# Softmax attention with a gated unit on one core: single score banks for VectorE, gate jobs that wait for weights, numbered PSUM banks in setup

## The chip, the cores and the metric

The kernel runs on one core of a Trainium2 chip. A core has TensorE (PE; its weight loads are a row of their own, PEld), VectorE (DVE), ScalarE (ACT), GpSimd (POOL) and SyncE (SP), each with its own instruction queue in program order, and 16 DMA engines. TensorE writes into PSUM, eight banks of 128 partitions x 512 floats. The metric is the device time of one execution in microseconds; what is shown is the median of three runs.

## The reference

The inputs are x (2048 x 640, bf16), the weights wqkv (640 x 1920) and wo (640 x 640) of an attention with 32 heads of 20 columns, and w_gate, w_up (640 x 1728) and w_down (1728 x 640).

```
xn  = layernorm(x)
q, k, v = split(xn @ wqkv)                      # 32 heads, 20 columns each
p   = softmax(q k^T / sqrt(20))                 # 2048 x 2048 for each head
s   = concat_heads(p v) @ wo
h   = sigmoid(xn @ w_gate) * (xn @ w_up)
g   = silu(h @ w_down)
out = x + s * g
```

The largest part is the softmax: 32 x 2048 x 2048 exponentials.

## The kernel before

**Setup.** Sixteen tiles of 128 rows of x are normalised, transposed on TensorE and copied to xnT. From it come K and q for the first group of four heads, and the first V tiles. The engines' order is a list of words written out by hand, ORDER: `tr.5` transposes tile 5, `k.2` multiplies a part of K, `kadd.2:DVE` evicts chunk 2 of K on VectorE, `qbound` and `qT` finish q. PSUM tiles come from rotating tags (`tp` with four buffers, `k` with three, `q` with one); `keep_clock` (L233) multiplies zeros into q's bank.

**Main part.** There are 32 passes: four chunks of 512 queries times eight groups of four heads. A pass has 64 *score banks* (16 key tiles x 4 heads), 128 keys x 512 queries each, so there are 2048 in all. A bank becomes exponentials in one of two ways:

- ScalarE takes them in *rounds*, three banks and two banks in turn (tiles `sc0` and `sc1`, five PSUM banks), one instruction each (L1166).
- VectorE takes one bank at a time, the tile `spare`, in four instructions (L1177, L1182, L1186, L1190): a bit trick with a cubic. In the program before, such a bank is issued only inside `issue()`, together with a ScalarE round, when less than 2500 ns of planned work lies before VectorE.

The exponentials are multiplied with V into the bank `oacc` (L1278, eight matmuls a batch, `P8` below). At the end of a pass `normalise` copies `oacc`, sends the denominators through DRAM and scales.

The two banks `misc0` and `misc1` are shared by `spare` and by all other products, the *jobs*: K, V and q of later groups, the bounds that keep the exponents in range (`bound_job`), gate and up (`gateup_job`, 56 of them), down, and the output. Jobs are generators; each yields what it needs next: a bank, a matmul, or a condition.

**What sets the order.** When the program is built, a planner walks through time. It keeps a time for TensorE (`pe[0]`) and queues with costs for ScalarE and VectorE, and at each step issues the next ScalarE round when it is due, else a batch with V, else a job's matmul, else a product with zeros that only keeps TensorE busy (`zero_add`, L1254). Nothing of this runs on the chip: what it leaves is each engine's fixed order and the semaphore waits for data and buffers. In the lists below a token such as `S3` or `S2` is a ScalarE round of that many score matmuls, `X1` a bank for VectorE. In the last pass a bank takes two matmuls of 256 queries, so the tokens read `S6` and `S4`.

**Weights of gate and up.** `load_glu` asks for the next job's weights on SP's queue when a job starts (two buffers each, `WB = 2`).

**The end.** The last pass is split into two halves of 256 queries. `last_job` handles the first half beside the last rounds: correction products (L855), VectorE's L868 and sums (L871). After the last exponential, VectorE copies the accumulator (L804), and a chain of a reciprocal, two small matmul steps and the last products ends with the output's DMA.

Of the kernel before, what the change touches and what calls it, by code (L numbers as in the profile page):

```python
# [9 lines left out]
FP32 = mybir.dt.float32  # L10
# [5 lines left out]
P = 128  # L16
# [21 lines left out]
apply.10 scale.14 apply.11 tr.7 stats.12 xnT.6 apply.14 less.12:DVE xnT.9 tr.10 xnT.7 sqrt.12  # L38
scale.12 tr.8 tr.11 xnT.10 xnT.11 k.1 xnT.8 apply.12 tr.14 stats.15 apply.13 tr.12 kmax.1
less.15:DVE sqrt.15 scale.15 xnT.14 xnT.12 tr.13 k.2 kmax.0 apply.15 kadd.0 tr.15 xnT.13:DVE xnT.15  # L40
k.3 k.4 qabs kmax.2 v.1 kmax.3 v.3 kmax.4 kmost v.0 kbound vd.1 vd.0 qbound kadd.1 table kadd.3:DVE
vd.3 v.2 vd.2 qT kadd.2:DVE
"""

LOG2E = 1.4426950408889634
# [13 lines left out]
def kernel(  # L59
# [99 lines left out]
    def v_matmuls(ps, tiles, h0, h1):  # L159
        n = (h1 - h0) * Dh  # L160
        for k, tt in enumerate(tiles):
            for kd in range(KD):
                nc.tensor.matmul(ps[:, k * n:(k + 1) * n], lhsT=xnT[:, kd, tt * P:(tt + 1) * P],  # L163
                                 rhs=wv[:, kd, h0 * Dh:h1 * Dh], start=(kd == 0), stop=(kd == KD - 1),
                                 skip_group_check=True)
                yield

    def v_copy(ps, tiles, h0, h1):
        n = len(tiles)
        nc.vector.tensor_copy(  # L170
            out=v_all[:, tiles[0]:tiles[0] + n, h0:h1, 1:1 + Dh],
            in_=ps[:, 0:n * (h1 - h0) * Dh].rearrange("p (t h e) -> p t h e", t=n, e=Dh))
# [3 lines left out]
    with tc.tile_pool(name="setup", bufs=1) as sp, \  # L176
# [53 lines left out]
        WARM, AFTER = 12, {0: 2, 1: 6, 2: 2, 3: 2, 4: 2, 5: 2}  # L230
        tps, kps, vps, first = {}, {}, {}, {}

        def keep_clock(n):  # L233
            if "idle" not in first:
                first["idle"] = ps0.tile([P, 512], FP32, tag="q", bufs=1, name="unused")
            for _ in range(n):
                nc.tensor.matmul(first["idle"].rearrange("p (k c) -> p k c", c=P), lhsT=zero,
                                 rhs=zero.unsqueeze(1).to_broadcast([P, 4, P]), start=True, stop=True)

        def copy(other, home, out, in_):  # L240
# [35 lines left out]
                                    scalar2=rstd[:, t:t + 1], op0=ALU.add, op1=ALU.mult)  # L276

        def transpose(t, other):
            tps[t] = ps0.tile([P, KD, P], BF16, tag="tp", bufs=4, name="tp")
            for kd in range(KD):  # L280
                nc.tensor.transpose(out=tps[t][:, kd, :], in_=x_sb[:, t, kd * P:(kd + 1) * P], identity=ident)
            keep_clock(AFTER.get(t, 0))

        def xnT_evict(t, other):
            copy(other, "ACT", xnT[:, :, t * P:(t + 1) * P], tps[t])
# [1 line left out]
        def k_mm(i, other):  # L287
            c, a, b = K_PARTS[i]
            if not a:
                kps[c] = ps0.tile([P, 512], FP32, tag="k", bufs=3, name="ps_k")  # L290
            first_matmuls(kps[c][:, a:b], wkp, slice(c * 512 + a, c * 512 + b))

        def k_part_max(i, other):
# [12 lines left out]
                                           op0=ALU.mult, op1=ALU.min)  # L306

        def v_mm(t, other):
            ps = ps0.tile([P, KD, P], BF16, tag="tp", bufs=4, name="ps_v")
            vps[t] = ps.rearrange("p k d -> p (k d)").bitcast(FP32)  # L310
            for _ in v_matmuls(vps[t], range(t, t + 1), 0, VF):
                pass

        def q_mm(t, other):
            first["ps"] = ps0.tile([P, 512], FP32, tag="q", bufs=1, name="ps_q")
            first_matmuls(first["ps"], wqp, slice(0, QC))

        def q_bound(t, other):
# [3 lines left out]
        def q_evict(t, other):  # L322
# [7 lines left out]
              "kmost": lambda t, other: k_most(DENSE, parts=len(K_PARTS)), "kbound": k_bound, "q": q_mm,  # L330
              "qabs": lambda t, other: first.update(abs=q_abs(first["ps"])), "qbound": q_bound,
              "table": lambda t, other: nc.scalar.activation(out=warm[:, 1:2], in_=eps_t, func=ACT.Exp),
              "qT": q_evict, "v": v_mm, "vd": lambda t, other: v_copy(vps[t], range(t, t + 1), 0, VF)}
        keep_clock(WARM)
        for word in ORDER.split():
            name, _, other = word.partition(":")
# [104 lines left out]
    def take_bank(name="work"):  # L441
        ready = [i for i in range(2) if banks[i].t is not None and banks[i].t <= pe[0]]
        if not ready:
            return None
        i = min(ready, key=lambda i: banks[i].t)
        banks[i] = Cell()
        return i, psum.tile([P, QC], FP32, tag=f"misc{i}", bufs=1, name=name)
# [7 lines left out]
    def give_bank(held, cell):  # L455
        banks[held] = cell
# [144 lines left out]
        next_pad[0] += 1  # L601
        return True

    glu_w = {}

    def load_glu(c, kf):
        fsz, f0 = fsz_list[kf], kf * P
        wg = glu[0].tile([P, KD, P], BF16, tag="wg", bufs=WB, name="wg")
        nc.sync.dma_start(out=wg[:, :, 0:fsz], in_=B_w_gate[:, f0:f0 + fsz].rearrange("(kd p) f -> p kd f", p=P))
        wu = glu[0].tile([P, KD, P], BF16, tag="wu", bufs=WB, name="wu")  # L610
        nc.sync.dma_start(out=wu[:, :, 0:fsz], in_=B_w_up[:, f0:f0 + fsz].rearrange("(kd p) f -> p kd f", p=P))
        glu_w[c, kf] = (wg, wu)

    hTs, h_cells, d_cells = {}, {}, {}

    def gateup_job(c, kf):
        fsz = fsz_list[kf]
        if kf == 0 and c:
            yield "known", lambda: len(d_cells.get(c - 1, [])) == QC // P
        elif kf:  # L620
            yield "known", lambda: c in hTs
        hT_free = d_cells[c - 1] if c and not kf else []
        n = c * NFT + kf + WB - 1
        if n < NQC * NFT:
            load_glu(n // NFT, n % NFT)
        wg, wu = glu_w.pop((c, kf))
        if kf == 0:
            hTs[c] = glu[0].tile([P, NFT, QC], BF16, tag="hT", bufs=1, name="hT")
        hT = hTs[c]
        cols = slice(c * QC, (c + 1) * QC)  # L630
        held, psg = yield "bank",
        for kd in range(KD):
            nc.tensor.matmul(psg[0:fsz, :], lhsT=wg[:, kd, 0:fsz], rhs=xnT[:, kd, cols],  # L633
                             start=(kd == 0), stop=(kd == KD - 1))
            yield "mm", MM5
        made = {}

        def gate():
            made["t"] = wk.tile([P, QC], BF16, tag="tnh", bufs=2, name="tnh")
            nc.scalar.activation(out=made["t"][0:fsz, :], in_=psg[0:fsz, :], func=ACT.Tanh, scale=0.5)  # L640

        gated = act.add(480.0, [Cell(pe[0] + PE_OUT + 100.0), *tnh_free[-2:-1]], gate, 0, EXP_LAG)
        give_bank(held, gated)
        held, psu = yield "bank",
        for kd in range(KD):
            nc.tensor.matmul(psu[0:fsz, :], lhsT=wu[:, kd, 0:fsz], rhs=xnT[:, kd, cols],  # L646
                             start=(kd == 0), stop=(kd == KD - 1))
            yield "mm", MM5
        tnh_free.append(dve.add(600.0, [Cell(pe[0] + PE_OUT), gated, *hT_free],
                                lambda: nc.vector.scalar_tensor_tensor(  # L650
                                    out=hT[0:fsz, kf, :], in0=made["t"][0:fsz, :], scalar=1.0,
                                    in1=psu[0:fsz, :], op0=ALU.add, op1=ALU.mult), 1))
        give_bank(held, tnh_free[-1])
        h_cells.setdefault(c, []).append(tnh_free[-1])
# [413 lines left out]

    KEEP_SPARE, KEEP_LATE, SPARE_END, next_round = 800.0, 400.0, 20 * PER_PASS, [0.0]
    BUFS, D_BACKLOG = {3: 4, 2: 4, 1: 3}, 2500.0  # L1070
    NEEDED, NEEDED_LAST = 6, 12
    PV_TIME = 2 * MM5 + 30.0
    sets = [Cell(0.0), Cell(0.0)]
    buffers = {n: [Cell(0.0)] * BUFS[n] for n in BUFS}
# [23 lines left out]
    def lacks():  # L1098
        return list({(w[1], w[2]): w for b in coming(GH) for w in needs(b)}.values())
# [8 lines left out]
    def dve_bank(banks):  # L1108
        b = min((x for x in coming(GH) if x not in banks), default=None)
        if b is None:  # L1110
            return None
        ends = PER_PASS * (b // PER_PASS + 1) if b < LAST else min(e for e in ENDS if e > b)
        if ends - b > (NEEDED if ends < NB else NEEDED_LAST):
            return b
        if ends == NB:
            return None
        b = ends + b % GH
        while b // GH in done_ahead[b % GH]:
            b += GH
        cells = [w[0].get(w[1]) for w in needs(b)]  # L1120
        if any(c is None or c.t is None or c.t > pe[0] for c in cells):
            return None
        return b
# [76 lines left out]
    def issue():  # L1200
# [23 lines left out]
        at_bank[0] += n  # L1224
        return n

    def pv_batch():

        p = pv_pass[0]
        if p >= len(steps) - 1 + len(PARTS):  # L1230
            return None
        if sum(pv_count[0]) == 0 and not (oacc_free[0].t is not None and oacc_free[0].t <= pe[0]):
            return None
        batch = []
        for j in range(GH):
            mine = []
            for x in ready_p[j]:
                b, buf, i = x
                if unit(b) > p or len(mine) == 2:
                    break  # L1240
                c, v = buf.made, v_cells.get((b % PER_PASS // GH, steps[min(p, len(steps) - 1)][1]))
                if c.t is not None and c.t + SEM <= pe[0] and v is not None and v.t is not None and v.t <= pe[0]:
                    mine.append(x)
            if len(mine) < 2:
                return None
            batch.append(mine)
        return batch
# [61 lines left out]
    while pv_pass[0] < len(steps) - 1 + len(PARTS):  # L1309
# [25 lines left out]
                continue  # L1335
        room = until - pe[0]
        next_round[0] = until
        held = sum(len(q) for q in ready_p)
        batch = pv_batch()
        cost = PV_TIME + (INTO["pv"] if mode[0] != "pv" else 0.0)  # L1340
# [102 lines left out]
```

## Time and profile before

| | |
|---|---|
| median of 3 runs | 891.46 us (891.35 to 891.49) |
| profiled execution, its own time | 894.59 us |
| its span | 892.9 us |
| TensorE busy | 813.2 us (91%) |
| VectorE busy | 839.8 us (94%) |
| ScalarE busy | 869.8 us (97%) |
| GpSimd busy | 162.6 us (18%) |
| granted TensorE clock, mean | 0.995 |
| DMA | 64.40 MB, 72 GB/s |

A group's line gives line, engine, operation, output and input with their shapes, the count, then the busy time and the mean duration of one, and then the engine's idle time just before these instructions, with what ended most of it. Busy time merges instructions that overlap, so it can be less than count times duration. Instruction times are from the span's start. A clock of 1.00 is TensorE's full speed.

### The profile page before, as it was taken

To read this page: it belongs to the slowest core of one execution; us is meant where nothing else is said; L and a number is where in the kernel's file an instruction comes from. 1 tells how busy PE (TensorE), PEld (TensorE's weight loads), DVE (VectorE), ACT (ScalarE), POOL (GpSimd) and SP (SyncE) were. 2 spreads that over 40 slices of the span, in tenths; PEclk is the share of its full clock that TensorE was granted. 3 is DMA by queue.
4 is the path that set the end of the run, shared out by engine and by line. 5 is a ranking of instruction groups with operands and counts; after the bars stand their busy time and mean duration, and the time that the engine had idled before them with its cause. 6 is when DMAs were issued, how large, how long until landed. Compare 5 with 4: busy or idle time off the path is not lost.

```text
span 892.9 us, 16976 instructions
## 1 busy us (share of the span) xinstructions
PE 813.2 (91%) x6259; PEld 291.3 (33%) x6343; DVE 839.8 (94%) x1482; ACT 869.8 (97%) x835; POOL 162.6 (18%) x311
## 2 busy tenths in 40 slices
PE   8899999999989899999899998989999898999896
PEld 3344333232223333232233332223333332233333
DVE  7799999999999999997999999999999989999997
ACT  7799999999999999999999999999999999999995
POOL 8401111011111212111101221101112220111121
PEclk9899999999999999999999999999999999999999
DMA  8113231135451134223202243303113433200012
GB/s 318 40 34 96 61 112 35 51 98 140 117 137 42 59 90 68 70 58 72 63 23 79 62 89 79 71 25 78 33 44 86 108 53 71 67 18 20 14 32 72
DMA packets 107673, 64.40 MB, mean 72 GB/s; under 512 B 80350, under 2 KB 101906, under 8 KB 107498
## 3 DMA queue, kind: packets, MB, share of 16 engines
q1 hardware_dynamic: 97382, 47.21, 19.9%
q0 software_dynamic: 10208, 16.11, 7.9%
q8 instruction: 49, 0.80, 0.4%
q14 instruction: 34, 0.28, 0.1%
HBM read 50.45 MB, written 16.13 MB: 75 GB/s over the span
## 4 chain that ended last, share of the span: by engine, by line
ACT 59%; issue 17%; PE 12%; DVE 8%; DMA 2%; POOL 0%; SPq 0%; DVEq 0%; ACTq 0%; POOLq 0%
ACT p L1166 55%; PE sc L1144 4%; ACT tnh L640 3%; DVE dy L1177 2%; PE oacc L1278 2%; PE work L137 2%; DVE du L1182 1%; DMA wqd<-in_A_wqkv_dram 1%; PE work L633 1%; DVE p L1190 1%; PE work L669 1%; ACT td L680 1%; DVE du L1186 1%; DMA den<-den_dram 0%; PE work L163 0%
## 5 line engine op out<-in xcount | busy, mean ns | idle before, releaser
L1166 ACT ACTIVATE p<-sc 128x1536 bf16<-128x1536 f32 x717 | 828.7, 1358 | 6.1 <-PE spare L1144 2.5
L1144 PE MATMUL sc<-qT,kT_all 21*128 21x512 bf16 (+1 forms) x1848 | 280.8, 377 | 57.4 <-ACT p L1166 48.1
L1177 DVE TENSOR_SCALAR dy<-spare 128x512 f32<-128x512 f32 x257 | 175.6, 684 | 24.7 <-PE spare L1144 22.2
L1144 PEld LDWEIGHTS <-kT_all 21*128 21x128 bf16 x2112 | 90.4, 91 | 288.3 <-issue 275.0
L1186 DVE SCALAR_TENSOR_TENSOR du<-du,dy 128x512 f32<-128x512 f32 x257 | 174.5, 682 | 1.7
L1190 DVE SCALAR_TENSOR_TENSOR p<-du,dy 128x512 uint16<-128x512 f32 x257 | 174.3, 681 | 1.4
L1182 DVE SCALAR_TENSOR_TENSOR du<-dy 128x512 f32<-128x512 uint16 x257 | 174.5, 683 | 0.8
L1278 PE MATMUL oacc<-p,v_all 128*21 128x512 bf16 (+1 forms) x2112 | 158.0, 377 | 0.6 <-DVE v_all L170 0.3
L1144 PE MATMUL spare<-qT,kT_all 21*128 21x512 bf16 (+1 forms) x264 | 99.0, 379 | 0.0
L762 POOL DMA_DIRECT2D den_dram<-oev x31 | 18.1, 584 | 392.6 <-DVE oev L761 392.6
L669 PE MATMUL work<-wd,hT 128*128 128x320 bf16 x448 | 85.5, 302 | 0.1
L633 PE MATMUL work<-xnT,wg 128*128 128x512 bf16 (+1 forms) x261 | 77.6, 383 | 1.9 <-issue 0.6
L646 PE MATMUL work<-xnT,wu 128*128 128x512 bf16 (+1 forms) x268 | 73.1, 381 | 1.2 <-DVE dy L1177 0.3
L778 POOL DMA_DIRECT2D rl<-rec_dram x124 | 62.1, 514 | 60.2 <-DMA rec_dram<-den 51.0
L1254 PE MATMUL oacc<-xnT,zero 128*128 128x512 bf16 x165 | 56.5, 387 | 3.5 <-issue 2.7
L1278 PEld LDWEIGHTS <-v_all 128*21 128x21 bf16 x2112 | 31.2, 90 | 62.6 <-issue 60.7
L669 PEld LDWEIGHTS <-hT 128*128 128x128 bf16 x448 | 35.0, 97 | 48.6 <-issue 39.1
L640 ACT ACTIVATE tnh<-work 128x512 bf16<-128x512 f32 (+1 forms) x56 | 41.2, 735 | 0.0
L650 DVE SCALAR_TENSOR_TENSOR hT<-tnh,work 128x512 bf16<-128x512 bf16 (+1 forms) x56 | 38.0, 678 | 2.2 <-ACT tnh L640 2.2
L772 POOL DMA_DIRECT2D rec_dram<-den x31 | 17.0, 549 | 123.0 <-DVE den L771 118.4
L708 PE MATMUL work<-wo_pad,oT 128*128 128x320 bf16 x192 | 35.6, 302 | 0.5 <-issue 0.5
L633 PEld LDWEIGHTS <-wg 128*128 128x128 bf16 (+1 forms) x280 | 21.7, 98 | 42.8 <-issue 31.1
(128 smaller groups left out, 562.5 us busy)
## 6 DMA issues: line engine op xcount, KB each, us to landing
wg<-in_B_w_gate_dram SPq DMA_DIRECT2D x52, 160.0 KB
wu<-in_B_w_up_dram SPq DMA_DIRECT2D x52, 160.0 KB
rl<-rec_dram POOLq DMA_DIRECT2D x124, 64.0 KB, 2.3
qT<-q_dram SPq DMA_DIRECT2D x31, 128.0 KB
gq_dram<-d POOLq DMA_DIRECT2D x12, 320.0 KB, 2.5
gqr<-gq_dram SPq DMA_DIRECT2D x12, 320.0 KB
kT_all<-k_dram SPq DMA_DIRECT2D x28, 128.0 KB
wd<-in_B_w_down_dram SPq DMA_DIRECT2D x13, 160.0 KB
```

What stands on the lines that cost most here:

```text
L633: nc.tensor.matmul(psg[0:fsz, :], lhsT=wg[:, kd, 0:fsz], rhs=xnT[:, kd, cols], start=(kd == 0), stop=(kd == KD - 1))
L640: nc.scalar.activation(out=made["t"][0:fsz, :], in_=psg[0:fsz, :], func=ACT.Tanh, scale=0.5)
L646: nc.tensor.matmul(psu[0:fsz, :], lhsT=wu[:, kd, 0:fsz], rhs=xnT[:, kd, cols], start=(kd == 0), stop=(kd == KD - 1))
L669: nc.tensor.matmul(psd[:, 0:HALF], lhsT=hT[0:fsz, kf, t4 * P:(t4 + 1) * P], rhs=glu[1][0:fsz, kf, e0_:e1_], start=(kf == 0), stop=(kf == N ...
L778: nc.gpsimd.dma_start(out=t["rl"][32 * j:32 * j + 32, :], in_=rec_dram[n, j:j + 1, :].to_broadcast([32, QC]))
L1144: nc.tensor.matmul(ps[:, c0:c0 + n], lhsT=kT_all[rows, g, kt * P:(kt + 1) * P], rhs=qTs[qc, g][rows, q0:q0 + n], start=True, stop=True, ti ...
L1166: nc.scalar.activation(out=buf.tile(), in_=ps, func=ACT.Exp, bias=EXP_BIAS, scale=exp_scale)
L1177: nc.vector.tensor_scalar(out=t["y"], in0=ps, scalar1=LEAST, scalar2=None, op0=ALU.max)
L1182: nc.vector.scalar_tensor_tensor(out=t["u"], in0=t["f"], scalar=CUBE_2, in1=t["f"], op0=ALU.add, op1=ALU.mult)
L1186: nc.vector.scalar_tensor_tensor(out=t["u"], in0=t["u"], scalar=CUBE_1, in1=t["f"], op0=ALU.add, op1=ALU.mult)
L1190: nc.vector.scalar_tensor_tensor(out=buf.tile()[:, 0, :].bitcast(U16), in0=t["u"], scalar=CUBE_SCALE, in1=t["y"], op0=ALU.mult, op1=ALU.add)
L1278: nc.tensor.matmul(oacc[32 * j:32 * j + 1 + Dh, q0:q0 + width], lhsT=v_all[:, kt, GH * g + j, 0:1 + Dh], rhs=buf.ap[:, i, c0:c0 + width], ...
```

## The change

Three things change.

1. A new function `alone` in the main loop. When the next round is not yet due, VectorE has less than 700 ns of planned work, and K, q and a PSUM bank are there, one score bank is issued for VectorE on its own, outside a ScalarE round.
2. A gate and up job waits, in the planner, until 4000 ns after its weights were asked for.
3. In setup each PSUM tile has a numbered bank: K's chunks take banks 0, 3, 1 and 0, the transposes and V take 4, 2, 5 and 6 in turn, q takes 7. V's first four tiles are made in two pairs instead of one by one. ORDER changes in its last two lines only: among others the copy of K's chunk 2 moves ahead of `qbound`, and four products with zeros into the bank of K's chunk 1 are added (`idle.3`, `idle.1`).

```diff
-k.3 k.4 qabs kmax.2 v.1 kmax.3 v.3 kmax.4 kmost v.0 kbound vd.1 vd.0 qbound kadd.1 table kadd.3:DVE
-vd.3 v.2 vd.2 qT kadd.2:DVE
+k.3 k.4 qabs kmax.2 kmax.3 kmax.4 v.0 idle.3 kmost kbound vd.0 kadd.2:DVE kadd.3:DVE qbound v.2
+idle.1 vd.2 kadd.1 table qT
...
-        def keep_clock(n):
-            if "idle" not in first:
-                first["idle"] = ps0.tile([P, 512], FP32, tag="q", bufs=1, name="unused")
+        K_BANKS, T_BANKS, Q_BANK = (0, 3, 1, 0), (4, 2, 5, 6), 7
+
+        def bank(n, name, dtype=FP32):
+            ps = ps0.tile([P, 512], FP32, tag=f"b{n}", bufs=1, name=name)
+            return ps if dtype == FP32 else ps.bitcast(dtype)[:, 0:D].rearrange("p (k c) -> p k c", c=P)
+
+        for n in range(8):
+            bank(n, "home")
+
+        def keep_clock(n, at=Q_BANK):
+            unused = bank(at, "unused")
...
-            for _ in v_matmuls(vps[t], range(t, t + 1), 0, VF):
+            vps[t] = bank(T_BANKS[t // 2], "ps_v")
+            for _ in v_matmuls(vps[t], range(t, t + 2), 0, VF):
...
-        glu_w[c, kf] = (wg, wu)
+        glu_w[c, kf], glu_t[c, kf] = (wg, wu), pe[0] + LANDED
...
             yield "known", lambda: c in hTs
+        yield "known", lambda: pe[0] > glu_t.get((c, kf), 1e18)
         hT_free = d_cells[c - 1] if c and not kf else []
...
+    def alone(room):
+        if (chunk[0] < 2 or (0.0 if mode[0] == "score" else INTO["score"]) + MM5 > room
+                or dve.backlog + max(0.0, dve.t - pe[0]) >= ALONE or any(c.t is None for c in d_made[-2:-1])):
+            return False
+        if any(w[0].get(w[1]) is None or w[0][w[1]].t is None or w[0][w[1]].t > pe[0] for w in lacks()):
+            return False
+        b = dve_bank([])
+        held = take_bank("spare") if b is not None else None
+        if held is None:
+            return False
+        pe_do("score", 0.0)
+        begun = pe[0]
+        score(held[1], b)
+        issued(b)
+        give_bank(held[0], dve_exp(held[1], b, begun))
+        pe_do("score", MM5)
+        at_bank[0] += 1
+        return True
...
         room = until - pe[0]
         next_round[0] = until
+        if b0 < NB and not stuck and alone(room):
+            idle = False
+            credit = min(credit + per_bank(b0), 3000.0)
+            continue
```

More of the change, by code (lines that the diff above doesn't have):

```diff
@@ L231 @@
         tps, kps, vps, first = {}, {}, {}, {}
-        def keep_clock(n):
-            if "idle" not in first:
-                first["idle"] = ps0.tile([P, 512], FP32, tag="q", bufs=1, name="unused")
+        K_BANKS, T_BANKS, Q_BANK = (0, 3, 1, 0), (4, 2, 5, 6), 7
[6 more added lines that the diff above has]
+            unused = bank(at, "unused")
             for _ in range(n):
-                nc.tensor.matmul(first["idle"].rearrange("p (k c) -> p k c", c=P), lhsT=zero,
+                nc.tensor.matmul(unused.rearrange("p (k c) -> p k c", c=P), lhsT=zero,
                                  rhs=zero.unsqueeze(1).to_broadcast([P, 4, P]), start=True, stop=True)
@@ L278, in transpose @@
         def transpose(t, other):
-            tps[t] = ps0.tile([P, KD, P], BF16, tag="tp", bufs=4, name="tp")
+            tps[t] = bank(T_BANKS[len(tps) % 4], "tp", BF16)
             for kd in range(KD):
                 nc.tensor.transpose(out=tps[t][:, kd, :], in_=x_sb[:, t, kd * P:(kd + 1) * P], identity=ident)
-            keep_clock(AFTER.get(t, 0))
+            if t in AFTER:
+                keep_clock(AFTER[t])
         def xnT_evict(t, other):
@@ L289, in k_mm @@
             if not a:
-                kps[c] = ps0.tile([P, 512], FP32, tag="k", bufs=3, name="ps_k")
+                kps[c] = bank(K_BANKS[c], "ps_k")
             first_matmuls(kps[c][:, a:b], wkp, slice(c * 512 + a, c * 512 + b))
@@ L308, in v_mm @@
         def v_mm(t, other):
-            ps = ps0.tile([P, KD, P], BF16, tag="tp", bufs=4, name="ps_v")
-            vps[t] = ps.rearrange("p k d -> p (k d)").bitcast(FP32)
-            for _ in v_matmuls(vps[t], range(t, t + 1), 0, VF):
+            vps[t] = bank(T_BANKS[t // 2], "ps_v")
+            for _ in v_matmuls(vps[t], range(t, t + 2), 0, VF):
                 pass
         def q_mm(t, other):
-            first["ps"] = ps0.tile([P, 512], FP32, tag="q", bufs=1, name="ps_q")
+            first["ps"] = bank(Q_BANK, "ps_q")
             first_matmuls(first["ps"], wqp, slice(0, QC))
@@ L332 @@
               "table": lambda t, other: nc.scalar.activation(out=warm[:, 1:2], in_=eps_t, func=ACT.Exp),
-              "qT": q_evict, "v": v_mm, "vd": lambda t, other: v_copy(vps[t], range(t, t + 1), 0, VF)}
+              "qT": q_evict, "v": v_mm, "vd": lambda t, other: v_copy(vps[t], range(t, t + 2), 0, VF),
+              "idle": lambda t, other: keep_clock(t, K_BANKS[1])}
         keep_clock(WARM)
@@ L602, in pads @@
         return True
-    glu_w = {}
+    glu_w, glu_t = {}, {}
     def load_glu(c, kf):
@@ L1070 @@
     BUFS, D_BACKLOG = {3: 4, 2: 4, 1: 3}, 2500.0
-    NEEDED, NEEDED_LAST = 6, 12
+    NEEDED, NEEDED_LAST, ALONE = 6, 12, 700.0
     PV_TIME = 2 * MM5 + 30.0
```

## The prediction

> **What bounds the kernel now.** I read the page's busy table and costliest groups, then busy time by stretches, then ScalarE's idle stretches in the timeline, then the two ends of the run.
>
> ```profile
> PE 813.2 (91%) x6259; PEld 291.3 (33%) x6343; DVE 839.8 (94%) x1482; ACT 869.8 (97%) x835; POOL 162.6 (18%) x311
> L1166 ACT ACTIVATE p<-sc 128x1536 bf16<-128x1536 f32 x717 | 828.7, 1358 | 6.1 <-PE spare L1144 2.5
> L1177 DVE TENSOR_SCALAR dy<-spare 128x512 f32<-128x512 f32 x257 | 175.6, 684 | 24.7 <-PE spare L1144 22.2
> L633 PE MATMUL work<-xnT,wg 128*128 128x512 bf16 (+1 forms) x261 | 77.6, 383 | 1.9 <-issue 0.6
> ```
>
> ScalarE is the bound: 717 exponential rounds hold 828.7 us of it. VectorE takes 257 single banks beside them (four instructions each) and waits 22.2 us for scores. The gate matmuls wait 1.9 us in all, and almost none of it for weights.
>
> ```profile
> 0.00:28.65 28.65, 22.69 (x161) 11.58 (x164) 22.01 (x72) 21.23 (x47) 24.34 (x59) 1.00 0.69 248
> 28.65:100.00 71.35, 66.10 (x536) 27.78 (x542) 66.52 (x119) 67.25 (x59) 8.38 (x18) 0.95 0.20 56
> 300.00:400.00 100.00, 92.95 (x711) 33.11 (x722) 97.40 (x169) 99.73 (x93) 19.93 (x35) 1.00 0.32 75
> 700.00:800.00 100.00, 90.21 (x677) 30.44 (x687) 90.22 (x153) 100.00 (x96) 18.33 (x32) 1.00 0.30 62
> 880.00:893.00 13.00, 5.66 (x47) 2.84 (x44) 7.84 (x16) 2.15 (x3) 0.40 (x1) 0.89 0.26 76
> ```
>
> The columns after the length are PE, PEld, DVE, ACT, POOL, the granted clock, DMA share and GB/s. From 128 us to 882 us ScalarE is full; nothing but fewer rounds shortens that stretch. Before it lie 28.65 us of setup and a start with holes, behind it a tail of 10.7 us. ScalarE's holes, one line for each stretch of it, the idle time before it in brackets:
>
> ```profile
> 28.65 2.37 ACT L1166 ACTIVATE p<-sc 128x1536 bf16<-128x1536 f32 x2 [1.56 <-PE sc L1144]
> 31.31 2.52 ACT L1166 ACTIVATE p<-sc 128x1536 bf16<-128x1536 f32 x2 [0.30 <-PE spare L1144]
> 35.68 8.54 ACT L1166 ACTIVATE p<-sc 128x1536 bf16<-128x1536 f32 x7 [1.84 <-PE spare L1144]
> 48.01 12.40 ACT L1166 ACTIVATE p<-sc 128x1024 bf16<-128x1024 f32 x11 [1.26 <-PE oacc L1278]
> ```
>
> With smaller ones (0.16, 0.40, 0.28, and 0.23 at 317 us) the holes after the first round make 4.47 us. The next rows show why two of them are there (PE busy time, instructions, then the clock):
>
> ```profile
> 23.40:26.80 3.40, 2.78 (x30) 1.00 0.00 0
> 26.80:30.20 3.40, 2.04 (x11) 0.98 0.06 14
> 30.20:33.60 3.40, 3.07 (x11) 0.50 0.11 19
> 33.60:37.00 3.40, 3.40 (x19) 0.52 0.12 36
> ```
>
> TensorE was busy 2.04 of 3.40 us at the hand-over from setup; then its clock was half for 6.8 us, and the holes of 0.30 and 1.84 us fall there.
>
> **The change part by part.** Counts are from the instruction order of the two built programs.
>
> *Rounds.* The new branch issues a bank for VectorE with no ScalarE round beside it. The programs have 13 such banks, and 249 beside rounds instead of 257: 262 in all, 5 more. ScalarE has 357 rounds of three banks and 357 of two instead of 358 and 358. A pair holds ScalarE for 828.7 / 358.5 = 2.31 us (durations of 1.573 and 1.145 us overlap). All of it lies on the path: **-2.31 us**. VectorE gets 5 x (0.684 + 0.683 + 0.682 + 0.681) = 13.65 us more. From 28.65 to 880 us it is busy 810.0 of 851.4 us by the stretches, so 41.4 us are free and 27.8 stay free. The cover is thinnest from 300 to 400 us, with 2.6 us free; about that stretch is rounds 240 to 320 (one in 1.19 us), which get 160 VectorE instructions instead of 157, so 2.0 us. TensorE has room: the zero products that only keep its clock fall from 215 to 185, 30 x 0.22 us (the spacing in a row of five, 1.25 us less 0.39 for one, over four) = 6.5 us, and in 132 places it waits 48.1 us for ScalarE. Cost there: nothing.
>
> *First round.* Before, the first scores wait for two VectorE evictions of K:
>
> ```profile
> 26.39 0.69 ACT L324 ACTIVATE qT<-ps_q,e_one 128x512 bf16<-128x512 f32 x1 [0.39 <-POOL v_all L346]
> 27.36 0.74 DVE L300 TENSOR_SCALAR kT_all<-ps_k,e 128x512 bf16<-128x512 f32 x1
> 28.16 0.39 PE L1144 MATMUL sc<-qT,kT_all 21*128 21x512 bf16 x3 [1.51 <-DVE kT_all L300]
> ```
>
> They need only chunk 0 of K and qT; they wait for the banks. In the new numbering the three-bank score tile lies on two transpose banks and q's bank, and the first score waits for qT alone. The bound is ready at 25.86 us as before: the VectorE work ahead of it is the same. On TensorE, V's two tiles (10 products, at 15 in 1.20 us) and three idle products (0.22 us each) reach from 24.24 to about 25.8 us, so the bound product stays at 25.92 us and qT ends at 27.08 us. What is late next is TensorE: ten V products from 26.14 us and one idle product, done issuing near 27.15 us. The first score moves from 28.16 to about 27.15 us: **-1.0 us**; the ends are 0 (another bank wait) and -1.08 us (qT). Behind it, the first K job waits for its bank until the second VectorE eviction of setup (about 27.0 us) and the first single for V's last copy (about 28 us), both before TensorE comes there.
>
> *Clock.* The new order has TensorE at ten V products and an idle one up to 27.3 us, scores and four K products to 28.5 us, two scores, a single and a K product to 29.1 us, and then the second three-bank round when the first exponential ends (27.65 + 1.57 us). From 26.8 to 30.2 us that is about 3.2 of 3.4 us, nearer the row with 2.78 (clock kept) than the row with 2.04 (clock lost). So I take **-2.14 us**, the two holes; the ends are 0 and -2.14. The other 2.33 us of holes I keep; by the same rows they could be 0 to 4.
>
> The Trainium skill ("TensorE: Matmul & The Clock Gate", Part 1) says that the clock drops after an idle window of some 3.4 us, and that the window runs freely, whatever the kernel does. The first half disagrees with this trace: the longest idle time here was 1.51 us. By the second half a dummy product could help one run and not the next; that is the first rival, which the sum by rows prices at 2.14 us.
>
> *Gate and up jobs.* They now start 4000 ns of the planner's time after their load was asked for; this is a condition in the planner, no instruction on an engine. There was no weight wait to remove: line L633's own list of waits, weight loads included, has 31.7 us of "issue" and 0.8 us behind weight DMAs. The first gate job moves from round 144 to round 154, the last from 637 to 635, and each chunk's down and out products follow. Loads go out 10 rounds later with them. SP and POOL issue as many instructions as before (323 and 316), in another order on SP, where a wait for a free qT buffer (up to 27 us) already stands without TensorE waiting for the tile. Cover: ScalarE is full there on rounds in either order. Cost 0, bounds -1.9 and +1.9 us.
>
> *V paired.* Four copies of 0.28 us become two of about 0.48 us: -0.16 us on VectorE in setup, inside the step above. 28 idle products only change their bank.
>
> *Tail.* The three last exponentials keep their sizes. But the first correction products of the last chunk stood one group earlier:
>
> ```profile
> 879.42 0.45 PE L855 MATMUL work<-wo_pad,oT 128*128 128x320 bf16 x2
> 879.80 0.39 PE L1144 MATMUL sc<-qT,kT_all 21*128 21x256 bf16 x4
> 879.90 0.49 DVE L868 SCALAR_TENSOR_TENSOR kT_all<-work,kT_all 128x320 f32<-128x320 f32 x1 [0.71 <-PE work L855]
> 882.68 0.41 DVE L804 COPY oev<-oacc 128x256 f32<-128x256 f32 x1
> ```
>
> Now they stand behind that S4 group, and VectorE has an 0.48 us part product, three of L868's and one sum before it may copy the accumulator: the same length of work (2.6 us), begun 0.7 us later. The last matmul ended before the copy, so VectorE sets it: **+0.7 us**, ends 0 and +1.0 (0.44 us more of VectorE work now lies between that copy and the reciprocal, against 0.32 us of slack).
>
> Sum: -2.31 - 1.0 - 2.14 + 0.7 = **-4.75 us**. The profiled execution took 894.59 us (span 892.9 and 1.7 around it) and would take 889.8; the median of the runs shown is 891.46, 3.13 less, and I take the same microseconds from it: **886.7 us**.
>
> **The rivals.**
>
> *The clock hole stays* (or was not in the timed runs, which are 3.13 us shorter than the profiled one). For it: those 3.13 us have no other cause in the profile. Against: the fuller row at the hand-over. 886.7 + 2.14 = 888.8 us.
>
> *A single ahead of a round blocks it.* TensorE works in order, and an extra bank outside a round stands ahead of the next one. If its bank is still held by VectorE's L1177, the round waits behind it, at most one such instruction: 0.68 us. With 13 of them that is 8.9 us: 895.6 us, slower than before. It undoes the gain from 0.37 us each on. For it: VectorE is 97% busy from 300 to 400 us, and three of the 13 come at rounds 286 to 325, 369 to 415 us. Against: the branch asks for an almost empty VectorE (under 700 ns planned), and before, TensorE waited for L1177 about 2 us in all.
>
> *The start runs clean.* The other holes shut too (up to 2.3 us, I take 1.4), with the tail at +0.4: 885.0 us. For it: the 1.26 us hole comes from a bound job that waits for VectorE in front of a round, and eight accumulations now stand before that job. Against: other jobs meet there in a new order.
>
> **How the numbers follow.** Forecast 0.50, clock hole 0.25, clean start 0.10, blocked rounds 0.15. A measurement here tells some 0.2% from no change, 1.8 us. Forecast, clock hole and clean start lie beyond that; of the blocked rounds, about half reach beyond 893.2 us and most of the rest end within 1.8 us of before: faster 0.84, same 0.09, slower 0.07. The range runs from the clean start, 885.0, to the clock hole with 1 us of new holes, 889.8.
>
> **What would show it.** First exponential near 27.65 us; clock at 1.00 from 27 to 37 us; holes after the first round near 2.3 us; 714 large rounds at unchanged durations and no hole from 130 us on; the copy of the last accumulator some 0.6 us later after the last exponential. It is wrong if the clock is half again after the hand-over, or if ScalarE shows waits for a spare bank or scores in the middle.

## The result

| | before | changed |
|---|---|---|
| median of 22 executions each, in turn on one chip | 892.66 us | 889.81 us |
| quickest | 891.35 us | 888.73 us |
| slowest | 897.7 us | 898.69 us |
| profiled execution, its own time | 894.59 us | 889.15 us |
| its span, mean granted clock | 892.9 us, 0.995 | 887.4 us, 0.999 |

The ratio is 0.997, 95% interval 0.9958 to 0.9983: 2.7 us faster (1.5 to 3.7). The forecast was 886.7 us, 4.75 us less than 891.46, the median of three executions; the median of 22 is 892.66. The direction was right, the size too large by three quarters.

The profile after, first the page: busy engines and the two groups that carry the change.

```profile
PE 804.4 (91%) x6238; PEld 289.4 (33%) x6316; DVE 852.3 (96%) x1500; ACT 866.5 (98%) x833; POOL 162.1 (18%) x311
L1176 ACT ACTIVATE p<-sc 128x1536 bf16<-128x1536 f32 x715 | 825.0, 1363 | 3.4 <-PE oacc L1307 2.2
L1187 DVE TENSOR_SCALAR dy<-spare 128x512 f32<-128x512 f32 x262 | 179.1, 684 | 14.0 <-PE spare L1154 10.9
```

715 rounds instead of 717 hold ScalarE for 825.0 instead of 828.7 us, 3.7 us less where one pair was priced at 2.31; why is open. VectorE took 262 single banks, was busy 12.5 us longer, and waited 10.9 instead of 22.2 us for scores.

ScalarE's holes, from its timeline (start, length, the idle time before in brackets); all that are listed after 27 us:

```profile
27.71 15.12 ACT L1176 ACTIVATE p<-sc 128x1536 bf16<-128x1536 f32 x13 [0.55 <-PE sc L1154]
43.44 3.28 ACT L1176 ACTIVATE p<-sc 128x1024 bf16<-128x1024 f32 x3 [0.60 <-PE oacc L1307]
48.32 92.17 ACT L1176 ACTIVATE p<-sc 128x1536 bf16<-128x1536 f32 x81 [1.60 <-PE oacc L1307]
397.35 2.37 ACT L1176 ACTIVATE p<-sc 128x1024 bf16<-128x1024 f32 x2 [0.17 <-PE sc L1154]
612.02 6.89 ACT L1176 ACTIVATE p<-sc 128x1024 bf16<-128x1024 f32 x6 [0.34 <-PE sc L1154]
668.38 0.74 ACT L690 ACTIVATE td<-d 128x640 bf16<-128x640 f32 x1 [0.20 <-DVE d L683]
```

The first round starts at 27.71 instead of 28.65 us, and the holes of 0.30 and 1.84 us near 31 and 35 us are gone. TensorE at the hand-over from setup (PE busy, instructions, clock, DMA):

```profile
23.40:26.80 3.40, 3.23 (x33) 1.00 0.00 0
26.80:30.20 3.40, 3.22 (x23) 1.00 0.10 21
30.20:33.60 3.40, 3.40 (x25) 1.00 0.08 15
33.60:37.00 3.40, 3.26 (x25) 1.00 0.36 111
```

From 26.8 us it is busy 3.22 us instead of 2.04, and the clock stays. The tail, by the timeline of VectorE: the last exponential ends at 875.85 us, and behind a later sum the copy of the accumulator comes 1.0 us after it (0.5 us before), the end of the span 11.55 us after it (10.74 before).

```profile
874.30 0.49 DVE L878 SCALAR_TENSOR_TENSOR kT_all<-work,kT_all 128x320 f32<-128x320 f32 x1 [1.98 <-PE work L865]
874.71 0.48 DVE L755 SCALAR_TENSOR_TENSOR hT<-work,kT_all 128x320 f32<-128x320 f32 x1
875.31 0.89 DVE L878 SCALAR_TENSOR_TENSOR kT_all<-work,kT_all 128x320 f32<-128x320 f32 x2
876.12 0.81 DVE L881 TENSOR_TENSOR ot<-kT_all,hT 128x640 bf16<-128x640 f32 x1
876.85 0.42 DVE L814 COPY oev<-oacc 128x256 f32<-128x256 f32 x1
```

So profile against profile the change is worth 5.44 us, and execution against execution some 2.7. That gap is what the experiments are about.

### The profile page after: what moved, and what is told of

It reads as the page before. It is cut to its first block, busy times and chain, and to the rows that moved or that the text cites. A ratio compares the mean times of both kernels' runs of the same rounds, so it can differ in the third digit from the quotient of the medians.

```text
span 887.4 us, 16929 instructions
## 1 busy us (share of the span) xinstructions
PE 804.4 (91%) x6238; PEld 289.4 (33%) x6316; DVE 852.3 (96%) x1500; ACT 866.5 (98%) x833; POOL 162.1 (18%) x311
## 4 chain that ended last, share of the span: by engine, by line
ACT 63%; issue 17%; PE 10%; DVE 8%; DMA 1%; POOL 1%; SPq 0%; ACTq 0%; DVEq 0%; POOLq 0%
ACT p L1176 58%; PE sc L1154 3%; ACT tnh L650 3%; PE oacc L1307 2%; PE work L679 2%; DVE du L1196 1%; DVE dy L1187 1%; DVE du L1192 1%; DMA wqd<-in_A_wqkv_dram 1%; DVE p L1200 1%; ACT td L690 1%; PE work L643 1%; PE work L656 1%; PE work L137 1%; DVE hT L660 1%
## 5 line engine op out<-in xcount | busy, mean ns | idle before, releaser
L1176 ACT ACTIVATE p<-sc 128x1536 bf16<-128x1536 f32 x715 | 825.0, 1363 | 3.4 <-PE oacc L1307 2.2
L1187 DVE TENSOR_SCALAR dy<-spare 128x512 f32<-128x512 f32 x262 | 179.1, 684 | 14.0 <-PE spare L1154 10.9
L1196 DVE SCALAR_TENSOR_TENSOR du<-du,dy 128x512 f32<-128x512 f32 x262 | 178.1, 683 | 2.1
L1200 DVE SCALAR_TENSOR_TENSOR p<-du,dy 128x512 uint16<-128x512 f32 x262 | 178.0, 682 | 1.3
L1192 DVE SCALAR_TENSOR_TENSOR du<-dy 128x512 f32<-128x512 uint16 x262 | 178.1, 683 | 0.8
L679 PE MATMUL work<-wd,hT 128*128 128x320 bf16 x448 | 83.5, 302 | 0.7 <-DVE dy L1187 0.7
L643 PE MATMUL work<-xnT,wg 128*128 128x512 bf16 (+1 forms) x259 | 75.2, 383 | 1.6 <-DVE hT L660 0.5
L1283 PE MATMUL oacc<-xnT,zero 128*128 128x512 bf16 x145 | 49.4, 384 | 3.3 <-issue 2.7
L656 PEld LDWEIGHTS <-wu 128*128 128x128 bf16 (+1 forms) x280 | 24.2, 98 | 38.1 <-issue 19.7
```

The costliest lines, as they stand in the source:

```text
L679: nc.tensor.matmul(psd[:, 0:HALF], lhsT=hT[0:fsz, kf, t4 * P:(t4 + 1) * P], rhs=glu[1][0:fsz, kf, e0_:e1_], start=(kf == 0), stop=(kf == N ...
L1176: nc.scalar.activation(out=buf.tile(), in_=ps, func=ACT.Exp, bias=EXP_BIAS, scale=exp_scale)
L1187: nc.vector.tensor_scalar(out=t["y"], in0=ps, scalar1=LEAST, scalar2=None, op0=ALU.max)
L1192: nc.vector.scalar_tensor_tensor(out=t["u"], in0=t["f"], scalar=CUBE_2, in1=t["f"], op0=ALU.add, op1=ALU.mult)
L1196: nc.vector.scalar_tensor_tensor(out=t["u"], in0=t["u"], scalar=CUBE_1, in1=t["f"], op0=ALU.add, op1=ALU.mult)
L1200: nc.vector.scalar_tensor_tensor(out=buf.tile()[:, 0, :].bitcast(U16), in0=t["u"], scalar=CUBE_SCALE, in1=t["y"], op0=ALU.mult, op1=ALU.add)
```

## The experiments

**Theory A.** The kernel before loses TensorE's clock at the hand-over in some executions only. The profiled one was of these; the three executions behind the 891.46 us were not. Then the 2.14 us were taken from a time that did not contain them. Below, an execution with a mean granted clock of 0.998 or more is called undisturbed. **Theory B.** The clock is lost there in every execution, and the changed kernel gives some 2 us back in another place. The runs below were made in three groups; those of one group share a chip and the executions of the kernel before.

### The kernel before, execution by execution

No edit. 

> The kernel before, unchanged, to see its executions one by one with span and granted clock. Theory A (the clock is lost at the hand-over from setup in some executions only, and the profiled one was such): its quickest executions are at 891.4 us with a mean clock of 0.998 or 0.999, and the others lie above in step with a lower clock; the profiled one, 894.59 us at 0.995, had 3.1 us of it. Theory B (the clock is lost at the hand-over in every execution, and the changed kernel gives back elsewhere what it wins there): the executions at 891.4 us have a clock of 0.995 or 0.996.

Its twelve executions, time and clock: 891.27 (0.998), 891.39 (0.999), 892.94 (0.997), 893.56 (0.996), 893.94 (0.998), 894.21 (0.994), 894.27 (0.995), 894.46 (0.994), 895.52 (0.994), 896.24 (0.993), 897.2 (0.990), 898.14 (0.990). The profiled one took 895.52 us, and its ScalarE timeline has the same two holes at the same places:

```profile
31.31 2.53 ACT L1166 ACTIVATE p<-sc 128x1536 bf16<-128x1536 f32 x2 [0.29 <-PE spare L1144]
35.68 8.54 ACT L1166 ACTIVATE p<-sc 128x1536 bf16<-128x1536 f32 x7 [1.84 <-PE spare L1144]
```

Over the three groups of runs with a clock for each execution there are 117 of the kernel before: 50 with 0.998 or more (median 891.49 us), 47 from 0.993 to 0.996 (median 894.71 us). The difference, 3.2 us, is about what stood between the first profile and the three times (3.13 us). The other 20 have 0.997 or less than 0.993. An estimate from the trace agrees: 6.8 us at half clock lower the mean clock of a span of 893 us by 0.004, about what lies between the two groups. So theory A fits. Two things stay open: one of the twelve took 893.94 us at 0.998, and only two profiles, this one and the first, show where such an execution of this kernel loses its clock.

### Setup alone, and the main part alone

The first has ORDER, the numbered banks and V in pairs, with the loop of before; the second has `alone` and the gate wait, with setup of before.

> Setup's part alone: numbered banks, V in pairs, idle products; the main loop's order is that of before (357 rounds of three... 358 pairs, 257 singles). Theory A: undisturbed executions gain the earlier first round only, 0.95 us (890.5 us), and executions with a lost clock become fewer. Theory B: undisturbed executions gain 0.95 + 2.1 us (888.3 us). The profile: first exponential near 27.7 us, no hole of 1.84 us at 35 us.

Median 891.29 us against 893.99 for the kernel before in this group; quickest 890.48 against 891.34, so -0.86 us where the clock is kept: near the 0.95 us of theory A, far from the 3 us of theory B. Only 2 of 12 executions have a clock under 0.998. The profile has the first exponential at 27.84 us, the clock at 1.00 throughout the hand-over, and no hole of 1.84 us:

```profile
27.84 12.81 ACT L1175 ACTIVATE p<-sc 128x1536 bf16<-128x1536 f32 x11 [0.55 <-PE sc L1153]
```

> The main part alone: single banks outside rounds and the gate wait, with setup as before. 262 singles, 357 pairs of rounds. Both theories: one pair of rounds less, -2.31 us, and the tail's later start, +0.8 us: 1.5 us less than before, about 889.9 us undisturbed; theory B has the hole at the hand-over in all of them, theory A in some.

Median 894.34 us; 11 of 12 executions have a clock from 0.987 to 0.995, where 23 of 35 of the kernel before in this group lie under 0.998. So the new loop alone does not keep the clock, and the new setup alone does in 10 of 12. The single other execution took 891.08 us, not 889.9. The profile shows the clock lost at the hand-over (holes of 0.93 and 1.22 us) and 1.6 us less than the profile of before, 893.0 against 894.59, near the 1.5 us expected. By its executions the main part alone is no gain: its price per round could be seen only in the profile.

### Without the idle products

```diff
-k.3 k.4 qabs kmax.2 kmax.3 kmax.4 v.0 idle.3 kmost kbound vd.0 kadd.2:DVE kadd.3:DVE qbound v.2
-idle.1 vd.2 kadd.1 table qT
+k.3 k.4 qabs kmax.2 kmax.3 kmax.4 v.0 kmost kbound vd.0 kadd.2:DVE kadd.3:DVE qbound v.2
+vd.2 kadd.1 table qT
```

> The changed kernel without its four products with zeros at the hand-over. Theory A: undisturbed executions as the changed kernel, 888.8 us, with a clock loss in more of them. Theory B: every execution loses the clock there and is about 2 us slower, 890.9 us. From 26.8 to 30.2 us TensorE would be busy some 0.25 us less, and from 23.4 to 26.8 us 0.7 us less than in the changed kernel.

Quickest 889.17 us, median 889.8; 9 of 12 executions have 0.998 or more (with the four products 17 of 22), and the profile has the first exponential at 27.70 us and no clock loss at the hand-over, with TensorE busy 3.09 of 3.40 us from 26.8 us. The four products are worth nothing that shows: the shorter wait for the first scores fills TensorE by itself.

### Only a filler at the hand-over of the kernel before

```diff
-vd.3 v.2 vd.2 qT kadd.2:DVE
+vd.3 v.2 idle.11 vd.2 qT kadd.2:DVE
```

`idle.11` are eleven 128 x 256 products with zeros into a transpose buffer. 

> The kernel before with one addition: eleven short products with zeros (some 1.2 us) after V's last product in setup, in the 1.5 us in which TensorE waits for VectorE there. Nothing else moves. If the idle TensorE at the hand-over is what costs the clock: undisturbed executions stay at 891.4 us (nothing on ScalarE's path is shorter), but executions near 894 to 895 us become few, the median falls from about 894 to about 891.6 us, and the profile shows a clock of 1.00 from 30 to 37 us and no hole of 1.84 us. If not: the median and the hole stay.

The hand-over in windows as above, and from the timeline ScalarE's first long stretch:

```profile
26.80:30.20 3.40, 3.10 (x20) 1.00 0.07 16
30.20:33.60 3.40, 3.24 (x27) 1.00 0.10 18
```

```profile
28.54 12.81 ACT L1172 ACTIVATE p<-sc 128x1536 bf16<-128x1536 f32 x11 [1.56 <-PE sc L1150]
```

The first round is as late as before, but the clock stays and both holes are gone. Two executions of 12 have a clock under 0.997; of the kernel before in the same group 15 of 35 have. So it is TensorE's idle time that costs the clock there, and the clock that makes the two holes. The median moved little, 892.51 against 893.01 us, because the undisturbed executions are at 891.8 to 893.0 us (median 892.15), 0.6 us above those of before (891.53). Why is open.

This profile shows one thing more: TensorE waits for the weights of the first gate job. The profiles of before and of the setup alone, with the same loop, have no such wait.

```profile
PE work L639 <- DMA wg<-in_B_w_gate_dram: 0.7, 1, 0.7
```

This wait made no hole on ScalarE, and the clock stayed at 1.00 around it.

This profile is also the fairer one to compare rounds with, though those 0.6 us may be in it: from the first exponential to the last it takes 850.83 us (28.54 to 879.37), the changed kernel 848.14 (27.71 to 875.85).

### Without the single banks, and without the gate wait

The first drops the call of `alone` in the loop, the second the one line `yield "known", lambda: pe[0] > glu_t...`.

> The changed kernel without the single banks outside rounds; the gate wait and setup stay. 259 singles, ScalarE 358 rounds of three and 357 of two: one round of three more than the changed kernel. At 0.46 us of ScalarE a bank, 3 x 0.46 = 1.4 us more than the changed kernel, 890.4 us undisturbed (changed kernel 889.0).

Quickest 890.91 us, 2.2 us more than the changed kernel's 888.73 (expected: 1.4). From the first exponential to the last its profile takes 850.73 us, 2.6 more, and its tail is 10.9 us, 0.65 less. The changed kernel did not run on this chip; beside the kernel before of its own group, whose quickest execution took 890.98 us, it gains next to nothing, though its first round starts at 27.58 us. And 7 of its 12 executions have a clock under 0.998; the profiled one has 0.999, so where they lose it is not shown.

> The changed kernel without the gate wait: 263 singles, 11 of them outside rounds, 357 rounds of three and 357 of two and no last round of one. If the gate wait only reorders: 0.4 us less than the changed kernel, 888.6 us undisturbed, and no TensorE time waiting for gate or up weights beyond 1 us. If the wait spares TensorE stalls on weights: the profile shows such stalls here.

This missed, and told most. The twelve executions stand in three heaps: four at 889.9 to 890.1 us (0.998 and more), three at 893.2 to 893.7 (0.992), five at 898.6 to 899.6 (0.982 to 0.986). The profile is of the last heap. TensorE's wait, its windows (one of 3.4 us, then four of ten), and ScalarE's waits:

```profile
PE work L642 <- DMA wg<-in_B_w_gate_dram: 1.7, 1, 1.7
```

```profile
196.60:200.00 3.40, 1.75 (x16) 0.98 0.95 214
190.00:200.00 10.00, 7.24 (x56) 0.99 0.43 103
200.00:210.00 10.00, 9.53 (x43) 0.50 0.38 106
210.00:220.00 10.00, 9.64 (x45) 0.50 0.24 57
220.00:230.00 10.00, 9.31 (x53) 0.81 0.43 107
```

```profile
ACT p L1175 <- PE sc L1153: 8.4, 10, 1.5
ACT p L1175 <- PE spare L1153: 1.5, 3, 0.6
```

Without the wait the first gate job stands in TensorE's queue before its weights have landed. TensorE waits 1.65 us, and after that the clock is half for some 24 us. ScalarE's waits in the last two lines all fall there but one (0.55 us, at the first round): twelve waits, 9.3 us in all. The first of them, 1.5 us, is the stall itself. That is as much as lies between this execution (899.25 us) and the first heap. Whether the executions of the first heap have the stall too is not shown. In the order of the built program, a wait for the first gate job alone gives the same order on TensorE, VectorE and ScalarE as the wait for all 56. No run was made of that, but the next one touches that job alone.

### The same, with TensorE kept busy while it waits

```diff
         held, psg = yield "bank",
+        for _ in range(8 if not c and not kf else 0):
+            nc.tensor.matmul(psg, lhsT=zero, rhs=xnT[:, 0, 0:QC], start=True, stop=True)
         for kd in range(KD):
```

> The kernel without the gate wait, with one addition: eight products with zeros (1.7 us) ahead of the first gate matmul, so that TensorE is busy while that job's weights land. Nothing else moves. If the idle time in front of the first gate job costs the clock there: the executions near 893.5 and 899 us vanish or become as rare as in the changed kernel, the profile shows a clock of 1.00 from 190 to 230 us and ScalarE waits of at most 2 us there instead of 8.8 us. If the waiting itself, or the DMA traffic, costs: holes of several us and executions near 899 us stay.

Ten of twelve executions at 889.4 to 890.05 us with 0.998 or more, the other two at 892.3 (0.995). The windows, and ScalarE's one hole there:

```profile
190.00:200.00 10.00, 9.09 (x65) 1.00 0.44 104
200.00:210.00 10.00, 9.25 (x66) 1.00 0.35 104
210.00:220.00 10.00, 9.42 (x70) 1.00 0.64 156
220.00:230.00 10.00, 9.23 (x69) 1.00 0.53 147
```

```profile
199.56 3.71 ACT L1177 ACTIVATE p<-sc 128x1536 bf16<-128x1536 f32 x3 [1.50 <-PE sc L1155]
```

The weights still hold up that job: its first matmul starts at 198.53 us (198.71 without the filler), and ScalarE still loses 1.50 us. The other 7.8 us and the heap at 899 us are gone. Here too it is the idle time that costs the clock.

### More single banks

```diff
-    NEEDED, NEEDED_LAST, ALONE = 6, 12, 700.0
+    NEEDED, NEEDED_LAST, ALONE = 6, 12, 2000.0
```

> The changed kernel with the limit of planned VectorE work raised from 700 to 2000 ns: 267 singles, 87 of them outside rounds, 356 pairs of rounds. If a single outside a round costs nothing: one pair less, 2.3 us less than the changed kernel, 886.7 us undisturbed (tail alike). If each delays the next round while its bank is still held (up to 0.68 us each), ScalarE shows holes, and at 0.05 us for each of the 74 more banks the gain is gone.

Slower than before: ratio 1.0025 (1.0008 to 1.0043), executions from 895.3 to 897.6 us. But not for the reason named. ScalarE's rounds fell to 823.0 us; its holes grew from 2.9 to 5.4 us, the longest where a round waits for an accumulation to free its buffer:

```profile
166.33 44.69 ACT L1176 ACTIVATE p<-sc 128x1536 bf16<-128x1536 f32 x39 [2.01 <-PE oacc L1307]
```

Waits of ScalarE for spare banks are 1.0 us in all. Of the 6.6 us that the profile's span is longer, 2.35 us lie between the first exponential and the last. The larger part is the tail, 15.6 instead of 11.55 us: a part product of six matmuls (L750) now lies between the copy of the accumulator and the reciprocal, 3.4 us apart instead of 1.9, and the output's transfer ended 5.5 us after VectorE's last sum instead of 3.1. What made that transfer longer was not looked into.

### The changed kernel again, and two attempts to better it

> The changed kernel once more, beside the other three on one chip: undisturbed executions at 888.7 to 889.5 us with a clock of 0.998 or more, about one in five slower with a lower clock, as in its first 22 executions.

888.92 us quickest, median 889.74 against 892.91, ratio 0.9972 (0.9956 to 0.9988), 9 of 12 executions at 0.998 or more. As the first time.

```diff
-                if c.t is not None and c.t + SEM <= pe[0] and v is not None and v.t is not None and v.t <= pe[0]:
+                if c.t is not None and c.t + SEM <= pe[0] and v is not None and v.t is not None and v.t + 600.0 <= pe[0]:
```

> The changed kernel with one condition changed: the planner lets a batch with V start 600 ns later after V's copy. 262 singles (9 outside rounds), 357 pairs, and the last correction products stand again ahead of the S4 group. If the two early holes (0.60 and 1.60 us before 50 us) come from batches that wait for V's copy ahead of a round: they shut, -2.2 us; with the tail of the kernel before, -0.8 us: 886.2 us undisturbed. If not: 888.3 us.

> As the run before it, with the limit of planned VectorE work at 500 instead of 700 ns: 262 singles, 7 of them outside rounds, and a similar tail. 886.2 us undisturbed, if what counts is the number of rounds, the early holes and the tail, and not how many singles stand outside rounds.

Both missed. The early holes did not shut (1.28 and 1.09 us, and 1.27 and 1.10, instead of 0.60 and 1.60). The first was slower than before, median 898.05 us: its profile loses the clock near 335 and 730 us, for about 3.4 us each time, and six of its 13 holes stand there (the changed kernel has six in all). Even its execution at 0.999 took 893.8 us. The second took 889.82 us at best, with 10 of 12 executions under 0.996; where those lose the clock was not looked into. One step did hold: with the correction products ahead of the S4 group again, the tail is 10.71 and 10.69 us, as in the kernel before (10.74).

## Why the prediction was wrong

- **The step that failed** is the last of the sum: "the median of the runs shown is 891.46, 3.13 less, and I take the same microseconds from it". Of the 4.75 us, 2.14 are the two clock holes, which the profiled execution had; the executions behind that median, by their length, had not (0.998 to 0.999 in executions of that length, 0.994 to 0.995 where the holes are). Without that term the same sum gives -2.6 us, and the runs give -2.7. That these meet so closely is in part luck: the -2.7 us also hold the rarer loss of the clock (5 of 22 and 3 of 12 executions under 0.998, against 58 of 105 of the kernel before). Undisturbed executions alone give -1.8 us by their medians (889.66 against the 891.49 of the later groups) and -2.1 us where both ran in one group (889.43 against 891.52), so the terms that are left are together 0.5 to 0.8 us too large. Which of them is open. The rival named it, "was not in the timed runs", with 888.8 us (the changed kernel's quickest execution took 888.73), and had a chance of 0.25: the 3.13 us between profile and median spoke for it and were given too little weight.
- **Clock.** As a mechanism it held: 3.22 of 3.40 us busy (forecast 3.2), clock kept, both holes gone, and a filler alone does the same. But the kernel before does not pay for it in each execution. The idle products were not needed. So its worth is in how often the slower executions come, not in the quickest ones.
- **Rounds.** Right in direction and near in size: -2.31 us forecast; -2.7 us from first to last exponential against the profile of before with a filler (850.83 to 848.14), which may hold 0.6 us of another cause.
- **First round.** Right: -0.94 us (forecast -1.0), with the first scores at 27.22 us (forecast 27.15).
- **Tail.** Right in size, +0.8 us (forecast +0.7), and only half by its reason: the copy of the accumulator came 0.5 us later, and the other 0.4 us lie between that copy and the reciprocal (1.88 us apart instead of 1.46), where the forecast saw slack for most of it. Two runs that put the correction products back have the tail at 10.7 us.
- **Gate wait.** Priced at 0, from "there was no weight wait to remove". True of the profile of before, but not of each execution of that loop: with the filler it waits 0.7 us for the first weights, at no cost on ScalarE. The single banks make another order, and in that one the wait removes a 1.65 us stall and the half clock behind it. The parts were priced one by one against the old order; a worth of the gate wait is shown only beside the single banks.
- **Other holes.** 2.33 us were kept; it is 2.91 us, and they were no longer the same ones.
- **The rival of blocked rounds** did not come: ScalarE has no wait for a spare bank in the changed kernel, and 1.0 us of them with 87 singles.
- **The free window.** That the window runs freely, as the Trainium skill has it ("TensorE: Matmul & The Clock Gate", Part 1), by which a product could help one run and not the next, agrees with executions of one kernel at 0.994 and 0.999; no run here isolates the phase.

## What to carry to other kernels

Before a term is taken from a time, ask whether that time contains it: a profiled execution 3 us above a tight median, with a clock of 0.995, is another execution than the timed ones, and a hole in it may not be in them. Where TensorE only feeds the engine that bounds, price an idle TensorE by the clock that it may lose and not by the wait: 1.65 us of waiting cost ScalarE 9.3 us. A guard that removes no wait in the old profile can still be what makes another part of the change safe, so look for its wait in the new order too.

## What the runs showed of the hardware

- One wait of 1.65 us on TensorE, in a window of 3.4 us in which it was busy 1.75 us, was followed by some 24 us at half clock, with TensorE busy 28.5 of the 30 us from 200 us on. At the hand-over of the kernel before, 2.04 of 3.40 us were followed by 6.8 us. With batches 600 ns later, the clock was half for about 3.4 us twice. The Trainium skill ("TensorE: Matmul & The Clock Gate", Part 1) has the clock return after at least one busy window of about 3.4 us; these four took seven, two, one and one.
- Executions of one kernel on one chip fall into heaps (889.9, 893.5 and 899 us without the gate wait) that follow the granted clock, with the same order of instructions in each.
